# Logits in a shared pool of six PSUM buffers, a third buffer of normalized tokens, and a new order of the pieces

## The chip, the cores and the metric

The kernel runs on one core of one Trainium2 chip. The metric is the time of one execution on the device in microseconds (us); lower is better. Times are medians of several runs of the same kernel. A profile is one further execution, recorded by the hardware; its span runs from the first to the last instruction.

Engine names in this text: PE multiplies matrices, DVE works on vectors, ACT evaluates functions and evicts PSUM, POOL (GpSimd) and SP mostly issue DMAs here. PSUM is the memory that PE writes.

## The reference

A transformer block on one sequence of S = 2048 tokens of width D = 640: a layer norm, then local dilated attention and an MLP side by side, and everything is added to the input.

```python
def _A_ref(x, wqkv, wo):
    H = 32; Dh = D // H                       # Dh = 20
    W, dil = 8, 2
    qkv = (x @ wqkv).reshape(B, S, 3, H, Dh)  # then transposed
    q, k, v = qkv[0], qkv[1], qkv[2]
    idx = pos[:, None] - (jnp.arange(W) * dil)[None, :]
    mask = idx >= 0
    logits = jnp.einsum("bhsd,bhswd->bhsw", q, kg) * scale   # kg: k at idx
    logits = jnp.where(mask[None, None, :, :], logits, -1e9)
    attn = _softmax(logits, axis=-1)
    o = jnp.einsum("bhsw,bhswd->bhsd", attn, vg)             # vg: v at idx
    return o.reshape(B, S, D) @ wo

def _B_ref(x, w1, b1, w2, b2):                # F = 1536
    h = _gelu(jnp.einsum("bsd,df->bsf", x, w1) + b1)
    return jnp.einsum("bsf,fd->bsd", h, w2) + b2

xn = _layernorm(x)
return x + _A_ref(xn, A_wqkv, A_wo) + _B_ref(xn, B_w1, B_b1, B_w2, B_b2)
```

Every token attends to itself and to the seven tokens 2, 4, ..., 14 places before it.

## The kernel before

**Chunks and blocks.** The 2048 tokens are four chunks (n = 0 to 3) of 512, each of four blocks (j or bl = 0 to 3) of 128. D = 640 is five channel tiles of 128. Most work happens with channels on the partitions and 512 tokens in the free dimension.

**Pieces and the order.** All work is cut into 647 named pieces, small functions that each emit a few instructions on one engine. One long string, ORDER, lists every piece once; the kernel calls them in that order with manual scheduling. So each engine's instruction stream is the sequence of its own pieces as they stand in ORDER, and each engine works through its stream in order. Semaphores make a piece wait for its operands and for the release of the buffer that it writes. An engine that waits holds up all that stands behind it.

**The pieces.** The first digit is the chunk.

- `st`, `su`, `sq`, `ng`, `rs`, `rc`: mean and variance of a block's tokens (DVE in chunks 0 and 1, ACT in 2 and 3), square root on ACT, reciprocal on DVE. `xn{n}{bl}`: the normalized block (L259), on DVE in chunk 0, on ACT after that, written to the pool `lnp`.
- `tp`, `tc0..`: transposes by PE and their copies (chunk 0 only). `tc{n}{bl}` of later chunks: a transposing DMA issued by SP (L292) that writes `xnT`, the normalized tokens with channels on the partitions.
- `ga`, `gb`, `gd`, `ge`, `hj`: q, k, v projections of chunk 0 in parts of 128 or 256 tokens (L349, L380); `gc`, `hc` their evictions by ACT. `pj{n}{which}{to}`: one output tile of q (0), k (1) or v (2) of later chunks, five matmuls of 128x512 (L336); `pc...` its eviction (L400).
- `qk{n}{j}{h}`: on DVE, the products of q with k at four of the eight window offsets (half h) for block j, into the tile `half` (L433). `pa{n}{j}{k}`: DVE folds the five channel tiles to two (KEPT = 2): one fold of 2048 elements (k = 0), one of 1024 (k = 1) (L465).
- `lg{n}`: 16 matmuls with the matrix `head_of` sum the channels of each head into the logits L (L474). `cl{n}`: ACT copies them to SBUF (L486). Softmax: `m`, `mx` (max and subtraction, DVE), `ex` (Exp on ACT), `ss`, `ri`, `at` (sum, reciprocal, product, DVE). `xd{n}{j}`: SP issues a DMA that spreads block j's weights over the channels (L548), to the tile `ax` in even chunks and to a spent part of `x_sb` in odd ones.
- `av{n}{j}{h}`: weights times v (DVE, L557). `aa{n}{j}`: the two halves are added, by an accumulating DMA that POOL issues in chunks 0 to 2 (L567) and by DVE in chunk 3 (L569). `ab`, `ot`: DVE adds the remaining four window offsets into `oT` (L573, L577).
- `f1{n}_{ft}`: a tile of the MLP's first layer, five matmuls of 128x512 (L586); `ge{n}_{ft}`: its Gelu on ACT (L602).
- `o{n}{bl}{pc}`: the output of block bl, in pieces: pc = 0 to 3 are three MLP tiles each, pc = 4 the attention's five tiles (which needs `ot` of that block); each a 512-wide `lo` and a 128-wide `hi` matmul (L622, L624). `oc`: two ACT copies; `od`: POOL issues a DMA that adds the block to the output.
- `xp`: x is written to the output; `xb`: POOL's DMA adds b2 to it; `ldx`, `ld2`, `ldo`: loads of x, w2, wo. `wa`, `wb`: small warming matmuls into a tile `idle`. `tb`, `b1`: b1 is transposed by PE and copied. The last block (33) ends with `oclo`, `ohi`, `ochi`, `ochd`.

**PSUM.** Three pools share it: `psA`, four buffers of 128x512 fp32, in which all projections, f1 tiles and PE transposes take turns; `psL`, one buffer of twice that size for the logits (and for `idle` and `tb` before them); `psO`, one `lo` and one `hi`. A buffer of `psA` is free again when ACT has evicted it.

**Tables.** ACT loads a function table (L173) whenever Sqrt, Gelu or Exp follows another of them.

The lines around the change, in the pools' part:

```python
psA = ctx.enter_context(tc.tile_pool(name="psA", bufs=4, space=bass.MemoryType.PSUM))
psL = ctx.enter_context(tc.tile_pool(name="psL", bufs=1, space=bass.MemoryType.PSUM))
lnp = ctx.enter_context(tc.tile_pool(name="lnp", bufs=2))
```

Of the kernel before, what the change touches and what calls it, by code (L numbers as in the profile page):

```python
# [31 lines left out]

KEPT = (2, 2, 2, 2)
BY_DMA = ((0, 1, 2, 3), (0, 1, 2, 3), (0, 1, 2, 3), ())
CUT = 2560
ACT_STATS = (2, 3)

COLS = ((0, 2), (2, 4), (4, 5))

ORDER = """  # L40
wa ho st00a sum1 st00 rs00 rc00 neg1 sq1 xn00a tp00a wb xn00b tp00b mean1 tc00a rs01 rc01 tb b1 tc00b ga gb2 xn01 tp01
tc01a tc01b gb3 gb4 gd ge gc4 gc1 hj100 st02a st02 rs02 hc100 st03a st03 hj101 gc0 rc02 xn02 rs03 hj102 rc03 xn03
hc101 hc102 tp02 tc02 hj202 tp03 tc03 hj201 hc201 hj010 st11a hc010 st13a hc202 st12a hj012 hc012 hj112 hc112 f10_3
st11 ldx hj011 f10_9 st10a st10 st12 st13 rs1 qk011 ge0_3 rc1 xn13 pad01 qk000 qk001 tc13 ge0_9 xn12 tc12 pa000 qk010
pk hj110 hc110 hj111 hc111 hc011 qk030 qk031 qk021 pad11 xn11 f10_10 tc11 pa010 xn10 qk020 tc10 ge0_10 f10_2 ge0_2
hj200 hc200 f10_0 pa030 f10_6 f10_11 su20 ge0_6 xp2 su22 su23 pj111 pc111 ge0_0 su21 ng2 pj110 pc110 pj104 pc104 sq23
pj120 pc120 ge0_11 sq20 pj114 pc114 pj113 pc113 pa001 pa020 pa021 pj102 pc102 pa031 pa011 lg0 cl0 mask m0 hj212 hc212
pj123 pc123 mx0 ex0 pj103 pc103 pj112 pc112 ss0 ri0 pj101 pc101 pj100 pc100 qk110 qk100 ld2 ldo xb2 sq22 qk130 pj124
pc124 hj211 sq21 qk121 rs2 pj121 pc121 hj210 hc210 rc2 f10_8 qk131 hc211 f11_9 ge1_9 xp0 xn20 f10_1 ge0_1 f10_7 tc20
f11_5 xb0 qk120 xn21 tc21 qk101 ge1_5 ge0_7 xn23 tc23 ge0_8 xn22 qk111 o000 f11_8 ge1_8 pa130 at0 pa110 f11_0 ge1_0  # L50
pa100 pad12 f10_5 ge0_5 f11_3 ge1_3 f11_6 su32 tc22 pa120 pa101 xd00 f10_4 su33 pj214 pc214 pa111 su31 su30 pj210
pc210 pad21 xd02 ge0_4 pj211 pa121 ge1_6 pa131 lg1 pj200 pad02 av000 av001 aa00 pc200 ng3 sq32 sq31 sq30 av020 pc211
av021 xd01 av011 o001 pj213 pc213 pj122 pj202 pc202 av010 o002 ab00 ot00 pj204 pj212 o003 pc212 pj223 pj222 cl1 aa02
xd03 pc122 av030 av031 m1 mx1 sq33 rs3 pj201 rc3 pc204 o004 oc00 ab02 ot02 pj224 ex1 o020 aa01 aa03 ss1 ri1 xn33 at1
ab01 ot01 ab03 o021 o022 o023 o024 xp1 tc33 pc201 xn32 tc32 pc222 oc02 ot03 od02 f12_7 xd10 av101 pad22 xd12 pc223
f11_4 xn30 o030 o031 o032 o033 pc224 xd11 xn31 pj221 av100 aa10 o034 oc03 f11_2 o010 ge1_4 tc31 av120 o011 o012 o013
o014 av110 av111 aa11 ge2_7 pc221 od03 f11_7 ge1_7 pj203 pc203 ge1_2 xd13 f11_1 av131 tc30 pj311 pc311 av130 aa13
pj304 f12_3 ge2_3 pj310 pc310 pc304 ge1_1 pj302 av121 aa12 ab10 ot10 f11_10 pc302 ge1_10 pj313 pc313 qk201 qk200 pj312
pj314 ab11 ot11 qk210 pc312 oc01 od01 f13_8 ge3_8 qk211 o130 ab13 pa200 pc314 f11_11 ge1_11 qk231 f12_6 o131 ot13
qk230 xb3 f12_0 ge2_0 pj220 pc220 o132 o133 o134 oc13 pj301 pc301 pa210 ge2_6 ab12 ot12 qk221 pj300 pj324 pc300 qk220  # L60
f13_7 xb1 pc324 od13 pa211 pj303 o120 pa230 pa220 pa231 pc303 pad31 pa221 pa201 lg2 ge3_7 cl2 qk301 f12_2 m2 mx2 ex2
f13_10 f12_8 ge2_8 o121 o122 o123 od00 o124 oc12 qk310 ss2 pj320 pc320 qk311 ri2 at2 xd22 xd20 o110 o111 qk331 o112
o113 o114 oc11 od11 qk330 f13_6 ge3_6 f12_5 ge2_5 ge3_10 o100 ge2_2 qk320 pa330 qk321 pa320 f13_5 f12_4 ge3_5 pj322
f13_2 o101 ge2_4 qk300 xd21 pc322 pa321 o102 o103 o104 ge3_2 pa300 pa301 pa331 pa310 pa311 lg3 f13_3 av210 f13_9 oc10
od10 od12 av211 aa21 ge3_3 f12_10 ge2_10 xd23 av230 av200 f12_1 ge2_1 ge3_9 av231 aa23 f12_9 ge2_9 f13_1 ge3_1 f13_4
f12_11 av201 av221 ab21 ge3_4 av220 pj321 o210 o211 o212 f13_0 ot21 ge2_11 o213 o214 f13_11 cl3 m3 mx3 ex3 pad32 ss3
ri3 at3 xd32 oc21 o200 o201 pc321 o202 aa20 ab20 ot20 ab23 ot23 ge3_0 aa22 o203 o310 o204 oc20 pj323 pc323 ab22 ot22
av320 o230 o231 o232 o233 o234 od20 oc23 av321 aa32 xd30 o311 o312 od21 ab32 o220 o221 o222 o223 o224 ge3_11 xd31
av311 od23 o313 av301 av310 oc22 od22 o320 o321 o322 o323 av300 ot32 o324 oc32 aa31 ab31 ot31 o314 oc31 o300 o301 o302
xd33 od32 aa30 o330 o303 ab30 ot30 o304 av331 av330 aa33 ab33 o331 o332 o333 ot33 od31 xl o334 oclo oc30 ohi ochi ochd  # L70
od30
""".split()


# [1 line left out]
def kernel(  # L76
# [16 lines left out]
    nc = tc.nc  # L93
# [5 lines left out]

    consts = ctx.enter_context(tc.tile_pool(name="consts", bufs=1))  # L100
    wts = ctx.enter_context(tc.tile_pool(name="wts", bufs=1))
    psA = ctx.enter_context(tc.tile_pool(name="psA", bufs=4, space=bass.MemoryType.PSUM))
    psL = ctx.enter_context(tc.tile_pool(name="psL", bufs=1, space=bass.MemoryType.PSUM))
    psO = ctx.enter_context(tc.tile_pool(name="psO", bufs=1, space=bass.MemoryType.PSUM))
    lnp = ctx.enter_context(tc.tile_pool(name="lnp", bufs=2))
    stp = ctx.enter_context(tc.tile_pool(name="stp", bufs=4))
    xtp = ctx.enter_context(tc.tile_pool(name="xtp", bufs=3))
    qkvp = ctx.enter_context(tc.tile_pool(name="qkvp", bufs=2))
# [9 lines left out]
    wqkv = [wts.tile([P, KT, D], BF16, name=f"w{s}_sb") for s in "qkv"]  # L118
# [6 lines left out]
    wqkv_v = A_wqkv.rearrange("(t p) n -> p t n", p=P)  # L125
# [6 lines left out]
    def load_w(s):  # L132
        nc.sync.dma_start(wqkv[s][:], wqkv_v[:, :, s * D : (s + 1) * D])
# [43 lines left out]
    mask = consts.tile([H, W, MW], BF16, name="mask")  # L177
# [16 lines left out]
    acc = consts.tile([P, NCH * BPC], F32, name="acc")  # L194
# [3 lines left out]
    tiles = {}  # L198
# [216 lines left out]
    half = prodp.tile([P, BPC, 2, W // 2, KT, P], BF16, name="half")  # L415
# [22 lines left out]
        )  # L438

    ones = nc.const_aps.tensor(1.0, [P, CH], BF16)  # L440
    idle = psL.tile([P, W, P], F32, tag="L", name="idle")

    def do_warm(n, cols):

        for _ in range(n):
            nc.tensor.matmul(
                idle[:].rearrange("p w c -> p (w c)")[:, 0:cols],
                lhsT=ones[:, 0:P],
                rhs=ones[:, 0:cols],
                start=True,  # L450
                stop=True,
            )
# [8 lines left out]
    def do_pa(n, j, k):  # L461

        a, b = ((slice(0, 2), slice(2, 4)), (slice(0, 1), slice(1, 2)), (slice(0, 1), slice(4, 5)))[k]
        kept, gone = (half[:, j, :, :, ts, :].rearrange("p h w t c -> p (h w) t c") for ts in (a, b))
        nc.vector.tensor_tensor(out=kept, in0=kept, in1=gone, op=ALU.add)  # L465

    def do_lg(n):
        L = psL.tile([P, W, P], F32, tag="L", name="L")
        tiles["L", n] = L
        ts = {KT: range(KT), 3: (0, 1, 4), 2: (0, 4), 1: (0,)}[KEPT[n]]  # L470
        for t in ts:
            for h in range(2):
                for j in range(BPC):
                    nc.tensor.matmul(  # L474
                        L[j * H : (j + 1) * H, W // 2 * h : W // 2 * (h + 1), :],
                        lhsT=head_of[:],
                        rhs=half[:, j, h, :, t, :],
                        start=(t == ts[0]),
                        stop=(t == ts[-1]),
                        skip_group_check=True,  # L480
                    )

    def do_cl(n):
        Lb = smp.tile([P, W, P], BF16, tag="Lb", name="Lb")
        tiles["Lb", n] = Lb
        nc.scalar.copy(Lb[:], tiles["L", n][:])  # L486

    def do_mask():
        Lb = tiles["Lb", 0]
# [74 lines left out]
    def do_aa(n, j):  # L564
        a, b = (half[:, j, h].rearrange("p w t c -> p (w t c)") for h in range(2))
        if j in BY_DMA[n]:
            nc.gpsimd.dma_start(a, b, accum_op=ALU.add, max_dma_last_dim=CUT)  # L567
        else:
            nc.vector.tensor_tensor(out=a, in0=a, in1=b, op=ALU.add)  # L569

    def do_ab(n, j):
        a, b = half[:, j, 0, 0:2], half[:, j, 0, 2:4]
        nc.vector.tensor_tensor(out=a, in0=a, in1=b, op=ALU.add)  # L573

    def do_ot(n, j):
        oT = get(("oT", n), lambda: otp.tile([P, KT, CH], BF16, tag="oT", name="oT"))
# [106 lines left out]
    piece("sum1", do_su, 0, 1)  # L683
    piece("neg1", do_ng, 0, 1, 2)
    piece("wa", do_warm, 1, P)
    piece("wb", do_warm, 2, P)
    piece("sq1", do_sq, 0, 1)
    piece("ga", do_ga, 0, 2)
# [99 lines left out]
```

## Time and profile before

| | |
|---|---|
| median of 3 runs | 207.28 us (207.03 to 208.06) |
| the profiled execution | 207.49 us, of which the span is 205.7 us |
| granted TensorE clock | 1.000 |
| DVE's longest groups | products `qk` 46.2 us (32 of 1.482), `av` 45.6 (32 of 1.485), folds `pa` 29.6, `ab` 13.1 |
| ACT's longest groups | Gelu 32.2 us (48 of about 0.685), casts of the projections 26.0, table loads 15.4 (12 of 1.283) |
| DMA queues | 31.77 MB, mean 154 GB/s |

The busy shares say how long an engine worked, not whether it set the time; the waits say who stood still for whom; the chain names, from the last instruction backwards, what each step had waited for. DVE's and ACT's instructions overlap at their ends: a product lasts 1.48 us, but the next one starts 1.40 us after it. For sums along an engine the distance from start to start is used. PE's 128x512 matmuls last 0.379 us each in the records and start every 0.216 us.

### The profile page before, as it was taken

Reading aid. Unit: us, or ns where it says so; the run is one execution under the profiler, and the core shown is the slowest. Engines: PE = TensorE matmul, PEld = TensorE weight load, DVE = VectorE, ACT = ScalarE, POOL = GpSimd, SP = SyncE. Lnnn points to the kernel's source line nnn. Section 1 sums busy time; section 2 is a strip of 40 time slices with the busy share of each in tenths; the row PEclk is TensorE's granted clock in tenths of the full one; section 3 lists DMA queues with packets and bytes.
Section 4 is the critical chain, followed back from the end, with each engine's and each line's share of the span. In section 5 each row is a group of like instructions: output and inputs, shape, how many; then the busy total and the mean of one; then the engine's idle time right before and its main releaser. Section 6 shows DMA issues by size and latency. Waiting matters only on the chain.

```text
span 205.7 us, 3262 instructions
## 1 busy us (share of the span) xinstructions
PE 200.8 (98%) x1285; PEld 112.2 (55%) x1285; DVE 175.4 (85%) x214; ACT 127.7 (62%) x242; POOL 34.4 (17%) x49
## 2 busy tenths in 40 slices
PE   7899999999999999999999999999999999999994
PEld 2797745565445555555555554555444555555552
DVE  3489999379998989949999994999979979799981
ACT  5488999899999879916466344834616854221210
POOL 2000000050000422102703303001023420311210
DMA  6999389969258599899996965018209998931244
GB/s 210 390 397 370 75 232 326 403 102 185 64 116 264 99 186 181 142 192 124 207 198 113 144 107 64 0 16 182 41 0 132 162 193 162 192 41 17 30 52 64
DMA packets 27335, 31.77 MB, mean 154 GB/s; under 512 B 9272, under 2 KB 22072, under 8 KB 27320
## 3 DMA queue, kind: packets, MB, share of 16 engines
q0 software_dynamic: 7408, 12.78, 39.4%
q1 hardware_dynamic: 19600, 18.58, 31.4%
q8 instruction: 10, 0.16, 0.3%
q10 hardware_dynamic: 312, 0.20, 0.3%
q14 instruction: 5, 0.04, 0.1%
HBM read 10.00 MB, written 7.54 MB: 85 GB/s over the span
## 4 chain that ended last, share of the span: by engine, by line
PE 95%; DMA 3%; SPq 0%; DVE 0%; issue 0%
PE lo L622 29%; PE hps L586 25%; PE pps L336 24%; PE hi L624 7%; PE gps L380 7%; DMA wq_sb<-in_A_wqkv_dram 3%; PE L L474 2%; PE gps L349 1%; PE tp L280 0%; SPq L130 0%; DVE osb L652 0%
## 5 line engine op out<-in xcount | busy, mean ns | idle before, releaser
L586 PE MATMUL hps<-xnT,w_sb 128*128 128x512 bf16 x240 | 55.6, 379 | 0.0
L433 DVE TENSOR_TENSOR half<-qT,kT 128x2560 bf16<-128x2560 bf16 x32 | 46.2, 1482 | 2.9 <-PE L L474 2.8
L622 PE MATMUL lo<-w_sb,hT 128*128 128x512 bf16 x144 | 41.3, 379 | 0.0
L586 PEld LDWEIGHTS <-w_sb 128*128 128x128 bf16 x240 | 22.9, 98 | 26.3 <-issue 0.8
L629 ACT CAST osb<-lo 128x512 bf16<-128x512 f32 x15 | 8.8, 587 | 36.8 <-PE hi L624 18.5
L624 PE MATMUL hi<-w_sb,hT 128*128 128x128 bf16 x144 | 31.5, 219 | 0.0
L602 ACT ACTIVATE hT<-hps,b1T 128x512 bf16<-128x512 f32 x36 | 24.0, 683 | 10.7 <-PE hps L586 10.7
L465 DVE TENSOR_TENSOR half<-half 128x2048 bf16<-128x2048 bf16 (+1 forms) x32 | 29.0, 952 | 0.2
L635 POOL DMA_DIRECT2D out_dram<-osb x15 | 13.6, 973 | 77.1 <-ACT osb L630 68.5
L557 DVE TENSOR_TENSOR half<-vT,x_sb 128x2560 bf16<-128x2560 bf16 x16 | 22.8, 1485 | 4.4 <-DMA x_sb<-e 3.0
L557 DVE TENSOR_TENSOR half<-vT,ax 128x2560 bf16<-128x2560 bf16 x16 | 22.8, 1485 | 2.3 <-PE L L474 1.4
L622 PEld LDWEIGHTS <-hT 128*128 128x128 bf16 x144 | 14.1, 98 | 16.8
L622 PE MATMUL lo<-wo,oT 128*128 128x512 bf16 x80 | 23.1, 379 | 0.0
L567 POOL DMA_DIRECT2D half<-half x12 | 14.3, 1195 | 48.9 <-DVE half L557 48.5
L336 PE MATMUL pps<-xnT,wv_sb 128*128 128x512 bf16 x75 | 18.5, 379 | 0.0
L336 PE MATMUL pps<-xnT,wq_sb 128*128 128x512 bf16 x75 | 18.3, 379 | 0.0
L336 PE MATMUL pps<-xnT,wk_sb 128*128 128x512 bf16 x75 | 17.7, 379 | 0.0
L624 PE MATMUL hi<-wo,oT 128*128 128x128 bf16 x80 | 16.9, 219 | 0.0
L173 ACT ACT_TABLE_LOAD x12 | 15.4, 1283 | 0.9 <-PEq L772 0.7
L624 PEld LDWEIGHTS <-hT 128*128 128x128 bf16 x144 | 14.1, 98 | 2.2
L573 DVE TENSOR_TENSOR half<-half 128x1280 bf16<-128x1280 bf16 x16 | 13.1, 820 | 1.3 <-DMA half<-half 1.2
L622 PEld LDWEIGHTS <-oT 128*128 128x128 bf16 x80 | 7.8, 98 | 9.4
(91 smaller groups left out, 263.7 us busy)
## 6 DMA issues: line engine op xcount, KB each, us to landing
half<-half POOLq DMA_DIRECT2D x12, 640.0 KB, 7.1
w_sb<-in_B_w_dram SPq DMA_DIRECT2D x4, 960.0 KB, 11.0
out_dram<-osb POOLq DMA_DIRECT2D x15, 160.0 KB, 4.0
ax<-e SPq DMA_DIRECT2D x8, 256.0 KB, 4.8
x_sb<-e SPq DMA_DIRECT2D x8, 256.0 KB, 4.8
out_dram<-b2bc POOLq DMA_DIRECT2D x3, 640.0 KB, 8.7
x_sb<-in_A_x_dram SPq DMA_DIRECT2D x1, 1280.0 KB, 12.9
out_dram<-x_sb SPq DMA_DIRECT2D x2, 640.0 KB, 8.7
```

The lines of the kernel that those rows point to most:

```text
L173: nc.scalar.activation(warm[:], nc.const_aps.tensor(0.0, [P, 1], F32), func)
L336: nc.tensor.matmul(ps[:], lhsT=wqkv_p[which][:, ti, to, :], rhs=xnT[:, ti, :], start=(ti == 0), stop=(ti == KT - 1),)
L380: nc.tensor.matmul(ps[:, to - a, :], lhsT=wqkv_p[which][:, ti, to, :], rhs=tiles["xnT", 0][:, ti, pair * 2 * P : (pair + 1) * 2 * P], star ...
L433: nc.vector.tensor_tensor(out=half[:, j, h], in0=q[:, :, at].unsqueeze(1).to_broadcast([P, W // 2, KT, P]), in1=window(k, h, at), op=ALU.mult,
L465: nc.vector.tensor_tensor(out=kept, in0=kept, in1=gone, op=ALU.add)
L557: nc.vector.tensor_tensor(out=half[:, j, h], in0=window(qkv_tile(n, 2), h, cs), in1=ax_view(n)[:, j, ws, :].unsqueeze(2).to_broadcast([P, ...
L567: nc.gpsimd.dma_start(a, b, accum_op=ALU.add, max_dma_last_dim=CUT)
L586: nc.tensor.matmul(ps[:], lhsT=w1_sb[:, ti, ft * P : (ft + 1) * P], rhs=tiles["xnT", n][:, ti, :], start=(ti == 0), stop=(ti == KT - 1),)
L602: nc.scalar.activation(hT, tiles["hps", n, ft][:], ACT.Gelu_apprx_tanh, bias=b1T[:, ft : ft + 1], scale=1.0)
L622: nc.tensor.matmul(lo[:], lhsT=lhs, rhs=rhs[:, 0:CH], start=first, stop=last)
L624: nc.tensor.matmul(hi[:, 0 : D - CH], lhsT=lhs, rhs=rhs[:, CH:D], start=first, stop=last)
L635: nc.gpsimd.dma_start(rows, tiles["osb", n, bl][:], accum_op=ALU.add)
```

## The change

Four things change.

1. `psL` is gone. `psA` has six buffers, and the logits take two of them, one for each half h of the window. `lg` runs over h outermost (before: over the channel tile), and `cl` copies each half by itself. `idle` and `tb` come from `psA` too.
2. `lnp`, the pool of normalized blocks, has three buffers where it had two.
3. ORDER is another permutation of the same pieces.
4. Some code is written otherwise to the same effect: `ab` flattens its operands; `AB_DMA` and `PA_DMA` could send folds to DMAs, but are empty; the load of the q weights is a loop of one step. KEPT is (2, 2, 2, 2) as before.

```diff
-    psA = ctx.enter_context(tc.tile_pool(name="psA", bufs=4, space=bass.MemoryType.PSUM))
-    psL = ctx.enter_context(tc.tile_pool(name="psL", bufs=1, space=bass.MemoryType.PSUM))
+    psA = ctx.enter_context(tc.tile_pool(name="psA", bufs=6, space=bass.MemoryType.PSUM))
     psO = ctx.enter_context(tc.tile_pool(name="psO", bufs=1, space=bass.MemoryType.PSUM))
-    lnp = ctx.enter_context(tc.tile_pool(name="lnp", bufs=2))
+    lnp = ctx.enter_context(tc.tile_pool(name="lnp", bufs=3))
...
-    idle = psL.tile([P, W, P], F32, tag="L", name="idle")
+    idle = psA.tile([P, CH], F32, tag="acc", name="idle")
...
-        tiles["tb"] = psL.tile([P, 2 * W * P], BF16, tag="L", name="tb")
+        tiles["tb"] = psA.tile([P, 2 * CH], BF16, tag="acc", name="tb")
...
     def do_lg(n):
-        L = psL.tile([P, W, P], F32, tag="L", name="L")
-        tiles["L", n] = L
+        tiles["L", n] = [psA.tile([P, W // 2, P], F32, tag="acc", name=f"L{h}") for h in range(2)]
         ts = {KT: range(KT), 3: (0, 1, 4), 2: (0, 4), 1: (0,)}[KEPT[n]]
-        for t in ts:
-            for h in range(2):
+        for h in range(2):
+            for t in ts:
                 for j in range(BPC):
                     nc.tensor.matmul(
-                        L[j * H : (j + 1) * H, W // 2 * h : W // 2 * (h + 1), :],
+                        tiles["L", n][h][j * H : (j + 1) * H, :, :],
...
-        nc.scalar.copy(Lb[:], tiles["L", n][:])
+        for h in range(2):
+            nc.scalar.copy(Lb[:, W // 2 * h : W // 2 * (h + 1), :], tiles["L", n][h][:])
...
     def do_ab(n, j):
-        a, b = half[:, j, 0, 0:2], half[:, j, 0, 2:4]
-        nc.vector.tensor_tensor(out=a, in0=a, in1=b, op=ALU.add)
+        a, b = (half[:, j, 0, w : w + 2].rearrange("p w t c -> p (w t c)") for w in (0, 2))
+        if j in AB_DMA[n]:
+            nc.gpsimd.dma_start(a, b, accum_op=ALU.add)
+        else:
+            nc.vector.tensor_tensor(out=a, in0=a, in1=b, op=ALU.add)
```

Of ORDER, some stretches in the new order (a line of "..." leaves out pieces):

```
ldx pad02 tb st00a wb st00 sum1 ho rs00 rc00 neg1 sq1 rs01 xn00a tp00a xn00b tp00b wa tc00a mean1 ga tc00b gb2 rc01
...
ge1_9 qk111 qk100 xn21 tc21 f10_4 qk121 pa120 pa121 f11_8 ge0_7 f10_5 pc124 xn22 ge1_3 f10_1 ge0_1 tc22 ge1_8 f11_5
...
pa100 qk110 ge0_4 pa110 pa111 pa131 pa101 lg1 cl1 av000 pj220 pc202 pj211 pc211 pj221 su33 su30 ng3 av001 aa00 xd02
...
pad21 o003 f12_11 sq31 rs3 pj122 pc122 m1 mx1 pj201 pc201 rc3 o004 oc00 av030 aa03 ex1 ab02 ot02 ss1 ri1 xn31 xn30
tc30 at1 xd10 ab01 ot01 pj212 pc212 xd11 ab03 ot03 pc223 o020 o021 o022 o023 o024 oc02 f12_7 pad22 o030 o031 o032 o033
xn32 pj222 xn33 xl av100 av101 od00 aa10 o034 pj203 xd13 av130 od02 oc03 o010 o011 o012 av110 pc222 av111 aa11 pc220
pc203 f11_7 ge1_7 o013 o014 tc31 tc32 f11_1 ge1_1 av131 tc33 pj311 pj310 pc310 xd12 pj303 av120 pc303 oc01 od01 av121
aa12 ab10 ot10 f12_5 ge2_11 f11_11 pc221 pj313 pc313 qk201 pj320 f12_0 pc311 ge2_5 pj304 pc304 qk200 pc320 pa200 pj302
...
ge2_6 o124 oc12 od12 m2 qk301 mx2 ex2 qk300 pj324 pc324 ss2 ri2 pj224 pc224 o110 o111 o112 o113 pa300 pa301 o114 oc11
od11 at2 xd23 xd21 qk310 pa310 f13_6 ge3_6 xd20 f12_3 ge2_3 qk321 f12_10 pa311 o100 o101 o102 xd22 pa320 o103 o104
oc10 pa321 f12_2 f13_8 pa330 pa331 ge2_10 lg3 cl3 av210
...
oc32 o300 o301 o302 od32 o303 o304 oc31 av330 oc30 o331 o332 o333 od31 aa33 ab33 ot33 o334 oclo ohi ochi od30 ochd
```

The same stretch of the order before, from the exponential of chunk 1 to its products, for comparison:

```
xd03 pc122 av030 av031 m1 mx1 sq33 rs3 pj201 rc3 pc204 o004 oc00 ab02 ot02 pj224 ex1 o020 aa01 aa03 ss1 ri1 xn33 at1
ab01 ot01 ab03 o021 o022 o023 o024 xp1 tc33 pc201 xn32 tc32 pc222 oc02 ot03 od02 f12_7 xd10 av101 pad22 xd12 pc223
f11_4 xn30 o030 o031 o032 o033 pc224 xd11 xn31 pj221 av100 aa10 o034 oc03 f11_2 o010 ge1_4 tc31 av120 o011 o012 o013
o014 av110 av111 aa11 ge2_7 pc221 od03 f11_7 ge1_7 pj203 pc203 ge1_2 xd13 f11_1 av131 tc30 pj311 pc311 av130 aa13
```

## The prediction

> **What bounds the kernel now.** I read the busy shares and the shares of the chain that ended last, then the waits of PE alone, then the chain in order of time.
>
> ```profile
> PE 200.8 (98%) x1285; PEld 112.2 (55%) x1285; DVE 175.4 (85%) x214; ACT 127.7 (62%) x242; POOL 34.4 (17%) x49
> ...
> PE 95%; DMA 3%; SPq 0%; DVE 0%; issue 0%
> ```
>
> ```profile
> PE tp L280 <- DVE xn L265: 0.8, 1, 0.8
> PE idle L446 <- PEq L772: 0.8, 1, 0.8
> PE gps L349 <- DMA wq_sb<-in_A_wqkv_dram: 0.6, 1, 0.6
> ```
>
> ```profile
> 1.20 5.51 DMA wq_sb<-in_A_wqkv_dram
> 6.76 1.03 PE gps L349 x15
> ...
> 202.00 0.96 PE hi L624 x17
> 202.99 0.29 DVE osb L652
> ```
>
> PE waits three times in the whole run, 2.2 us together, and all three lie before 6.76 us, where the first q projection finds its weights. From there to 202.95 PE is never idle. So the span is 6.76 (load), 196.2 (matmuls back to back) and 2.8 (last eviction and store). No order of the same matmuls makes the middle shorter; the new one can only open holes in it. The question is whether every matmul still finds its operand and its PSUM buffer in time.
>
> **The change, part by part.** The matmuls are the same in number and form: 0 us. The head: `tb` now stands before the first transposes on PE and waits for b1, whose last descriptor lands at 5.24; xn00a ends at 5.38 and wq lands at 6.71, so the start stays 6.76: 0, bounds 0 and +0.3 (b1 later by as much). The tail (o334, ohi, ochi, its store) is unchanged: 0. Eviction of the logits, from the groups of instructions:
>
> ```profile
> L486 ACT CAST Lb<-L 128x1024 bf16<-128x1024 f32 x4 | 4.0, 1012 | 0.8 <-PE L L474 0.8
> L400 ACT CAST qT<-pps 128x512 bf16<-128x512 f32 x15 | 8.7, 588 | 2.6 <-PE pps L336 2.6
> ```
>
> One cast of 1.012 becomes two of 0.588: 0.16 us more ACT time per chunk, but with h outermost the first half is complete after 8 of 16 matmuls, 0.49 us sooner (16 take 0.98). It lies on the softmax chain and gains some 0.3 us there; PE sees none of it, because the next chunk's products cover it.
>
> The order: I place each matmul piece by the row it had, plus the pieces that moved ahead of it, minus those that moved behind. One f1 or pj piece is 5 matmuls in 1.08, an o piece of three is 0.81, five gps matmuls are 0.55. lg1: 63.85 + 2 x 1.08 - 0.81 = 65.2. pj311: 100.95 - 1.08 = 99.87. o134: 119.32 + 3 x 1.08 = 122.56. lg2: 126.98 + 2 x 1.08 - 0.81 = 128.33. lg3: 151.90 + 1.08 = 152.98. o334 stays at 200.76. Against each I set the work of the engine that feeds it, with the start-to-start steps of the DVE rows (product 1.40, or 1.52 where the next instruction needs it; first fold 1.14 or 1.25; second fold 0.61; ab and ot 0.86 and 0.41, 0.52 if needed next).
>
> lg0 and lg1 keep their room: DVE has the last fold at about 36.3 against 37.0, and 64.7 against 65.2. The tightest stretch is chunk 1's softmax. These are SP's and then DVE's timelines there:
>
> ```profile
> 82.66 2.60 SPq L292 DMA_TRANSPOSE xnT<-xn  x2
> 85.35 3.25 SPq L548 DMA_DIRECT2D x_sb<-e  x3
> 88.69 2.76 SPq L292 DMA_TRANSPOSE xnT<-xn  x1
> 91.50 0.58 SPq L548 DMA_DIRECT2D x_sb<-e  x1
> 92.14 2.48 SPq L292 DMA_TRANSPOSE xnT<-xn  x1
> ```
>
> ```profile
> 84.36 0.69 DVE L531 TENSOR_TENSOR e<-e,rs 128x1024 bf16<-128x1024 bf16 x1
> ...
> 90.58 9.90 DVE L557 TENSOR_TENSOR half<-vT,x_sb 128x2560 bf16<-128x2560 bf16 x7 [3.01 <-DMA x_sb<-e]
> ...
> 128.12 1.49 DVE L433 TENSOR_TENSOR half<-qT,kT 128x2560 bf16<-128x2560 bf16 x1 [2.83 <-PE L L474]
> ```
>
> The attention weights of a chunk go out in four spreads (xd); DVE stands still for 3.01 us until the first has landed. Before, three spreads, one transpose, the fourth spread, one transpose. New: xd10, xd11, xd13, then three transposes (tc31, tc32, tc33), and only then xd12. ex1 comes 0.96 later (o004 ends at 79.4 instead of 78.5, then table load and warm), so at1 ends at 86.0. SP then issues the three spreads (3.34 with the gaps) until 89.4. Three transposes at the rows' 2.76, 2.48 and, with no spread in flight any more, 1.22 (the shortest issues) end near 96.0; bounds 3 x 1.2 and 3 x 2.76, so 93.1 to 97.7. xd12 lands 4.8 later (median of the spreads; 3.5 to 6.2): 100.8, bounds 96.6 to 103.9. DVE starts chunk 1's products when xd10 lands, 86.05 + 5.2 = 91.3, and needs xd12 after six of them, at 99.7. It waits 1.1, bounds 0 and 4.2. From there to the end of pa201 the steps sum to 27.1: 126.8 plus the wait, 127.9, against lg2 at 128.33. So 1.5 us of the wait is free and the slack absorbs it: 0 on PE, bounds 0 and +2.7. pj311 needs tc33 (issued near 94.8, 2.4 to 5.9 to landing, so 97.2 to 100.7) at 99.87: 0, bounds 0 and +0.8, not additive, since a late PE gives DVE the same time back.
>
> On this queue the Trainium skill speaks against the row: "DMA: Bandwidth & Descriptors", Issuing engines are not separate DMA queues, calls the time a sequencer takes to start a DMA usually small relative to the DMA itself. By that, xd12 would be out by 90 and nothing would wait. The rows show 1.2 to 2.8 us per transpose issue against 2.4 to landing, so the sum goes by the rows.
>
> After lg2 the chain is: oc12 at 136.2, 0.75 for its two casts, 1.40 to the Exp, 1.06 for it, then DVE from ss2 to the end of pa331, 13.3: 152.8 against lg3 at 152.98. Nearly a tie. The other DVE meetings have 0.5 us or more (ot21 166.4 against o214 166.9; ot22 184.6 against o224 185.2), and ot33 comes 3 us before o334 (1.5 before). The accumulating DMAs (aa) are issued at about the old distance from their readers: 0.
>
> PSUM: six buffers carry what four and a dedicated pair did. I checked each matmul piece against the eviction that frees its buffer, with ACT laid out the same way. Closest: f10_1 at 55.38 behind ge0_7 ending at 55.27, pj220 0.15 after pc200, pj313 0.2 after ge2_11, o030 0.1 after oc02, hj010 0.2 after tc03, all 0 if the rows hold. For six such meetings and lg3 I allow 0.3 us in all, 0.05 each, an estimate: the casts' starts scatter that much behind the matmuls. Bounds 0 and +1.2 (below). The third buffer of normalized tokens only lets ACT write a third block before the first has been transposed: 0, since PE has 1.08-us pieces to run meanwhile.
>
> Sum: 205.7 + 0.3 = 206.0 of span; with the 1.8 us around it (this execution took 207.49) 207.8. It was 0.2 above the median of 207.28, so against the median 207.6.
>
> **The rivals.** SP's queue decides (slower): the three transposes keep 2.76 each because the spreads are still in flight, and xd12 lands at 97.7 + 5.2 = 102.9. DVE waits 3.2, pa201 ends at 130.0, lg2 is 1.7 late; it decides from a landing after 101.2. Time 207.3 + 0.3 + 1.7 = 209.3. For it: both transposes behind a spread took 2.5 to 2.8. Against: the pair with none ahead took 2.60 together.
>
> ACT becomes the bound through the shared buffers (slower): from ge0_2 at 20.5 to 55.3 ACT has some 60 rows with hardly a gap, and it meets f10_1 with 0.1 us to spare. If its rows run 3% longer than laid out, that is 1.0 us there, and PE stands it out: 208.6. It decides from 0.1 us. For it: ACT is above 80% busy in the slices to 55 us. Against: in the kernel before, meetings of 0.1 to 0.2 us cost PE nothing.
>
> The clock drops (slower): the fourteen warm matmuls at the start take 3.87 us where warm steps would give 10 x 0.216 + 4 x 0.055 = 2.4. A hole that cools the array costs such a 1.5: 207.6 + 1.5 = 209.1. Against: the longest hole above is under 3 us, and the granted clock is 1.000 although PE paused three times at the start. The Trainium skill, "TensorE: Matmul & The Clock Gate", A second HAM failure mode, describes a kernel whose cycling through PSUM banks made PE idle briefly and often until the clock fell back. No run here shows it.
>
> Faster: only what lies outside the 196.2 us can shrink. If the start came when xn00's transposes are copied, at 6.6, it would save 0.2; beyond 1.0 nothing in the rows offers it.
>
> **How the numbers follow.** A measurement of this kernel can tell about 0.5% (1.04 us) from no change. Forecast, no hole over 1 us: 0.63, own range 206.9 to 208.3. SP's queue 0.16, ACT 0.12, clock 0.03, faster 0.05; the last 0.01 is a mishap I don't see, put with slower. That gives slower 0.32, same 0.63, faster 0.05. The range reaches from 206.9 (nothing lost, low end of the scatter) to 209.2, which takes in ACT's case and most of the queue's.
>
> **What would show it.** Right: PE's waits are still the three at the start, each later one below 0.3; xd12's issue stands behind three transposes at 95 to 97; DVE waits near 100 for a spread and lg2 starts at 128.3 to 128.6; PE ends near 203. Wrong: a wait of PE for half at lg2 or lg3 of over 1 us, waits for casts or for xnT summing to 1 us, 128x512 matmuls longer than 379 ns, or a first projection well off 6.76.

## The result and the profile after

| | before | after |
|---|---|---|
| median | 207.32 us (206.99 to 208.06, 6 runs) | 209.83 us (209.16 to 210.58, 6 runs) |
| ratio | | 1.0116, 95% interval 1.0097 to 1.0135 |
| the profiled execution | 207.49 us, span 205.7 us | 209.45 us (one of the six), span 207.6 us |
| granted TensorE clock | 1.000 | 1.000 |

The change made the kernel 1.2% slower, 2.5 us by the medians. In this and the later runs the ratios leave out single executions over 1.5% above the fastest of their kernel (214.21, 214.52 and 213.34 us in three of the later kernels); medians and ranges count them. The two profiled executions lie 1.9 us of span apart; the rest is that the one of after lies 0.4 below its median and the one of before 0.2 above. So the trace has to explain 1.9 us.

The busy shares of the kernel after, and the shares of the chain that ended last:

```profile
PE 202.1 (97%) x1285; PEld 112.4 (54%) x1285; DVE 176.6 (85%) x214; ACT 127.0 (61%) x246; POOL 34.6 (17%) x49
...
PE 74%; DVE 12%; ACT 7%; DMA 4%; issue 2%; SPq 0%; DVEq 0%
```

Before, 95% of the chain was PE. Now it leaves PE for a quarter of the span. PE's waits in the kernel after (who waits for whom: us in total, times, the longest):

```profile
PE lo L631 <- DVE oT L586: 1.4, 1, 1.4
PE idle L449 <- PEq L781: 0.8, 1, 0.8
PE L L479 <- DVE half L471: 0.3, 1, 0.3
PE gps L352 <- DVE mv L240: 0.2, 1, 0.2
```

Two of them are new and lie in the stretch where PE used to run without a gap: an output projection (o134) that waits for `ot13`, and the logits lg2 that wait for DVE's last fold. From the starts of the matmuls, the holes are 1.53 us ahead of o134 (122.54 to 124.07), 0.34 at lg2 and 0.27 at pj100 (a transpose that lands at 30.42). The first q projection starts 0.18 sooner than before (6.58; its weights landed at 6.34). Together 1.53 + 0.34 + 0.27 - 0.18 = 1.96: the whole difference, to 0.1 (the spans differ by 1.85, the two times by 1.96).

Where the chain turns off is seen in the same chain in order of time (start, length, what):

```profile
94.34 0.21 SPq L295
94.56 0.05 issue
94.61 8.33 DMA x_sb<-e
102.94 0.02 issue
102.96 0.04 DVE half L563
103.00 1.37 issue
104.37 1.48 DVE half L563
```

One spread of the attention weights, issued at 94.61, takes 8.33 us to land. SP's timeline of the kernel after says which (start, length, what, how many):

```profile
84.50 1.99 SPq L295 DMA_TRANSPOSE xnT<-xn  x1
86.59 3.24 SPq L554 DMA_DIRECT2D x_sb<-e  x3
89.87 4.69 SPq L295 DMA_TRANSPOSE xnT<-xn  x3
94.61 1.73 SPq L554 DMA_DIRECT2D x_sb<-e  x1
```

It is xd12, behind three transposes. And DVE's timeline there (in brackets the idle time before, and who ended it):

```profile
91.21 8.50 DVE L563 TENSOR_TENSOR half<-vT,x_sb 128x2560 bf16<-128x2560 bf16 x6 [0.60 <-DMA x_sb<-e]
102.96 2.89 DVE L563 TENSOR_TENSOR half<-vT,x_sb 128x2560 bf16<-128x2560 bf16 x2 [3.25 <-DMA x_sb<-e]
```

DVE makes six products, stands still for 3.25 us until xd12 is there, and everything behind it on DVE is that much late. About 1.4 us of it is slack; 1.53 + 0.34 reach PE.

Why 8.33, where the kernel before had no spread above 6.2? The view of the DMA queues, for the kernel after from 96.6 to 100 us and then from 100 to 103 (packets, MB, share of the 16 engines; q0 carries GpSimd's transfers, q1 SyncE's):

```profile
q0 software_dynamic: 259, 0.66, 101.8%
q1 hardware_dynamic: 148, 0.03, 5.4%
```

```profile
q1 hardware_dynamic: 142, 0.26, 59.7%
q0 software_dynamic: 174, 0.23, 45.4%
```

POOL's timeline has the accumulating transfer aa10 (640 KB), first in the kernel before, then in the kernel after, where the output rows od02 (160 KB) follow it:

```profile
93.77 1.20 POOL L567 DMA_DIRECT2D half<-half  x1 [7.52 <-DVE half L557]
```

```profile
94.40 1.20 POOL L573 DMA_DIRECT2D half<-half  x1 [10.81 <-DVE half L563]
95.11 1.44 POOL L644 DMA_DIRECT2D out_dram<-osb  x1
```

So POOL issued aa10 at 94.40, 0.2 us ahead of xd12; before, it came 2.3 us behind the last spread (91.50). Until 100 us its 0.66 MB have the engines nearly to themselves (packets overlap, so a share can pass 100%); SyncE's queue moves 0.03 MB. Only then come the 0.26 MB of xd12. That is a reading; the experiments test it.

### The profile page after: what moved, and what is told of

It reads as the page before. It is cut to its first block, busy times and chain, and to the rows that moved or that the text cites. A ratio compares the mean times of both kernels' runs of the same rounds, so it can differ in the third digit from the quotient of the medians.

```text
span 207.6 us, 3272 instructions
## 1 busy us (share of the span) xinstructions
PE 202.1 (97%) x1285; PEld 112.4 (54%) x1285; DVE 176.6 (85%) x214; ACT 127.0 (61%) x246; POOL 34.6 (17%) x49
## 4 chain that ended last, share of the span: by engine, by line
PE 74%; DVE 12%; ACT 7%; DMA 4%; issue 2%; SPq 0%; DVEq 0%
PE lo L631 25%; PE pps L339 16%; PE hps L595 15%; PE hi L633 6%; DVE half L436 6%; PE gps L383 5%; DMA x_sb<-e 4%; DVE half L471 4%; PE idle L449 2%; PE L L479 2%; ACT xn L266 2%; DVE half L582 1%; PE gps L352 1%; ACT hT L611 1%; ACT trash L224 1%
## 5 line engine op out<-in xcount | busy, mean ns | idle before, releaser
L631 PE MATMUL lo<-w_sb,hT 128*128 128x512 bf16 x144 | 40.7, 379 | 0.0
L471 DVE TENSOR_TENSOR half<-half 128x2048 bf16<-128x2048 bf16 (+1 forms) x32 | 29.5, 953 | 0.5
L644 POOL DMA_DIRECT2D out_dram<-osb x15 | 14.3, 996 | 71.0 <-ACT osb L639 71.0
L339 PE MATMUL pps<-xnT,wq_sb 128*128 128x512 bf16 x75 | 17.7, 379 | 0.1
```

Source lines behind the costliest of these rows:

```text
L339: nc.tensor.matmul(ps[:], lhsT=wqkv_p[which][:, ti, to, :], rhs=xnT[:, ti, :], start=(ti == 0), stop=(ti == KT - 1),)
L631: nc.tensor.matmul(lo[:], lhsT=lhs, rhs=rhs[:, 0:CH], start=first, stop=last)
L644: nc.gpsimd.dma_start(rows, tiles["osb", n, bl][:], accum_op=ALU.add)
```

## The experiments

Two theories stood at the start. Theory 1: the order of SyncE's queue, with xd12 last and just behind aa10. Theory 2: the shared pool of six banks with the logits in two tiles. The steps named are pieces of ORDER; a moved piece changes its place in its engine's queue, and its instructions stay the same.

### The spread ahead of the transposes; past one transpose only

```diff
-xn32 pj222 xn33 xl av100 av101 od00 aa10 o034 pj203 xd13 av130
+xn32 pj222 xn33 xl av100 av101 od00 aa10 o034 pj203 xd13 xd12 av130
...
-tc33 pj311 pj310 pc310 xd12 pj303 av120
+tc33 pj311 pj310 pc310 pj303 av120
```

> The changed kernel with one step moved: the spread xd12 goes ahead of the three transposes tc31, tc32, tc33 on SyncE's queue, straight behind xd13. Theory 1 (xd12 is issued last, behind three transposes and just behind the accumulating transfer aa10; av120 waits for its landing, and TensorE pays at o134 and lg2): xd12 is issued near 89.9 instead of 94.61 and lands near 94 to 95 instead of 102.94, VectorE's wait of 3.2 us before av120 is gone, o134 and lg2 start without a hole, and the time is 209.8 - 1.53 - 0.34, about 207.9. Theory 2, the rival (the shared pool of six banks and the logits cut into two tiles make TensorE late, and VectorE's wait is slack): the wait goes and the time stays, 209.5 to 210.

Measured: 211.93 us (210.49 to 214.21), ratio 1.0206, interval 1.0166 to 1.0246. Slower still, and neither theory had that. PE's waits and SP's timeline of this kernel:

```profile
PE pps L339 <- DMA xnT<-xn: 2.8, 1, 2.8
PE idle L449 <- PEq L781: 0.8, 1, 0.8
```

```profile
84.80 2.10 SPq L295 DMA_TRANSPOSE xnT<-xn  x1
87.00 4.88 SPq L554 DMA_DIRECT2D x_sb<-e  x4
91.92 6.83 SPq L295 DMA_TRANSPOSE xnT<-xn  x3
```

The first half of the forecast holds: xd12 lands at 95.58, DVE's wait is gone, and so are the holes at o134 and lg2. But now the last transpose, tc33, is last on the queue, issued at 95.70 behind aa10 (95.06); it lands 7.1 us later at 102.82, and PE waits for it at pj311 (due near 99.9). The wait was handed on.

```diff
-tc31 tc32 f11_1 ge1_1 av131 tc33 pj311 pj310 pc310 xd12 pj303
+tc31 tc32 f11_1 ge1_1 av131 xd12 tc33 pj311 pj310 pc310 pj303
```

> The changed kernel with the spread xd12 moved past one transpose only, between tc32 and tc33 on SyncE's queue, so that it is issued near 93.0, some 1.4 us ahead of the accumulating transfer aa10 (issued 94.40). Theory 1a (xd12 lands late because its packets wait for all of aa10's on the 16 DMA engines): it lands near 97 to 98, before av120 wants it (99.7), VectorE's wait is gone, about 207.9. Theory 1b (only its place on the queue counts): it lands earlier by what it is issued earlier, 1.6, so near 101.3; VectorE still waits 1.6, TensorE loses 0.2 to 0.4 of the 1.87, about 208.3 or more. Theory 2 (pool and cut logits): 209.5 to 210.

Measured: 210.04 us (209.03 to 214.52), ratio 1.0123, interval 1.0085 to 1.0162. xd12, issued at 92.95 with aa10 at 94.14, lands at 96.56: 3.6 us, as theory 1a said (1b: 101.3). tc33, issued at 93.66, lands 7.9 us later at 101.59, and PE waits 2.4 for it. The time (about 207.9 was forecast) was wrong for the same reason as in the run before: I had not asked what is last next.

### The code without the order

```diff
-ldx pad02 tb st00a wb st00 sum1 ho rs00 rc00 neg1 sq1 rs01 xn00a tp00a xn00b tp00b wa tc00a mean1 ga tc00b gb2 rc01
+wa ho st00a sum1 st00 rs00 rc00 neg1 sq1 xn00a tp00a wb xn00b tp00b mean1 tc00a rs01 rc01 tb b1 tc00b ga gb2 xn01 tp01
...
```

> The changed kernel's code (six shared banks, logits in two tiles, three buffers of normalized tokens) with the written order of the kernel before. Theory 1 (the order of the spreads): as fast as before, 207.0 to 207.6. Theory 2 (pool and cut logits): TensorE waits for banks in the old order too, 209 or more. If both have a part, it lies between, near 208.4.

Measured: 207.2 us (207.01 to 209.56), ratio 1.0006, interval 0.9982 to 1.0031. Theory 2 falls. Six shared banks, the cut logits and the third buffer cost nothing in the old order, so the 2.5 us come with the new one. That they cost nothing together with the new order either is shown by the run without aa10 below, which has both.

### The kernel before, with its last spread later

```diff
-pj203 pc203 ge1_2 xd13 f11_1 av131 tc30 pj311
+pj203 pc203 ge1_2 tc30 xd13 f11_1 av131 pj311
```

> The kernel before with one step moved: the transpose tc30 goes ahead of the spread xd13 on SyncE's queue, so that the fourth spread is issued near 94, just behind the accumulating transfer aa10 (issued 93.77) instead of 2.3 ahead of it (91.50). Nothing of the shared pool is in it. Theory 1: xd13 lands near 102 instead of 95.81, av131 (which ran at 97.6) waits some 4.5, the second chunk's logits lose their margin of 1.69 and come 2 to 3 late, 209.2 to 210.2. Theory 2 (pool and cut logits are to blame): VectorE's slack takes the wait, 207.3 to 207.8.

Measured: 207.12 us (206.95 to 209.94), ratio 1.0002, interval 0.9987 to 1.0017. The forecast of theory 1 (209.2 to 210.2) missed, but where the two transfers can be seen, the edit did not do what it was made for. In its profiled execution av100 started 1.9 us later than before, aa10 moved with it to 95.66, and xd13 (94.67) was still 1.0 us ahead; it landed at 98.42, after 3.75 us. That execution is the slowest of the thirteen (209.94 us): its first q projection came at 7.42 instead of 6.76, the granted clock was 0.50 from 7.86 to 11.27 us, and everything behind ran some 2 us late. Which of the two transfers goes first in the other twelve is not shown, so this run decides nothing.

### aa10 moved, and aa10 left out

```diff
-av101 od00 aa10 o034 pj203 xd13 av130 od02 oc03 o010 o011 o012 av110 pc222 av111 aa11 pc220
+av101 od00 o034 pj203 xd13 av130 od02 oc03 o010 o011 o012 av110 pc222 av111 aa11 aa10 pc220
```

> The changed kernel with one step moved on GpSimd's queue: the accumulating transfer aa10 (640 KB) goes behind aa11, so that it is issued near 99.8 instead of 94.40 and is not on the 16 DMA engines when the last items of SyncE's queue are (tc33 issued 93.33, xd12 issued 94.61). SyncE's queue is untouched. Theory 1a (what is issued last on SyncE, spread or transpose, lands 7 to 8 us after its issue because aa10's 640 KB go first; the two kernels with xd12 moved forward only handed this to tc33): xd12 lands near 98.6 instead of 102.94, tc33 near 96, av120 starts without a wait at 99.7, o134 and lg2 have no hole, about 207.9. Theory 1b (the issue times on SyncE alone are to blame): the landing stays near 102 and the time near 209.8. In either case ab10 may wait for aa10 up to 1.5 us on VectorE, in front of ot10.

Measured: 214.88 us (214.49 to 215.25), ratio 1.0365, interval 1.0342 to 1.0387. The landing came as theory 1a has it: xd12, issued at 96.62 with no aa10 about, lands at 100.20, 3.6 us later, and DVE runs through its products. The time came out 7 us wrong, because aa10, now queued behind aa11, itself landed 8.9 us after its issue (100.73 to 109.61), and DVE's next instruction needs it. DVE's waits in this stretch:

```profile
DVE half L582 <- DMA half<-half: 6.1, 2, 5.8
DVE half L563 <- DMA x_sb<-e: 1.4, 1, 1.4
```

I had allowed 1.5 us for the first line. It can't be used to price the change; leaving the transfer out can.

```diff
     def do_aa(n, j):
+        if (n, j) == (1, 0):
+            return
```

> The changed kernel without the transfer aa10: the halves of the second chunk's first prompt are not added, so its output is not the reference's there. Everything on SyncE stays. It takes one suspected cost away by itself. Theory 1a (aa10's 640 KB go ahead of the fourth spread on the 16 DMA engines): xd12 is issued near 94.6 as before and lands near 98 to 98.6 instead of 102.94; VectorE does not wait at av120, o134 and lg2 have no hole: 209.8 - 1.9, about 207.9. If what delays xd12 is the transposes ahead of it and not aa10, it lands near 102 and the time stays at 209.8.

Measured: 207.53 us (206.98 to 207.99), ratio 1.0008, interval 0.9991 to 1.0024. SyncE's queue has the changed kernel's order, three transposes ahead of xd12 and all, and xd12 is issued even later, at 96.11; yet it lands at 99.60, 3.5 us after. The DMA queues of this kernel from 96.1 to 99.6 us show SyncE's alone:

```profile
q1 hardware_dynamic: 661, 0.39, 60.3%
```

DVE's eight products run in one stretch, and PE loses nothing at o134 and lg2:

```profile
92.30 11.31 DVE L563 TENSOR_TENSOR half<-vT,x_sb 128x2560 bf16<-128x2560 bf16 x8 [1.37 <-DMA x_sb<-e]
```

With this transfer gone, the loss of the new order is within the error of nothing. One more thing moved with it: od02, which stands behind aa10 on POOL's queue, went out at 86.25 instead of 95.11 (in the run with aa10 behind aa11, at 86.83). It is not the cause: in the kernel after, the 0.66 MB up to 100 us are aa10's 640 KB alone, and od02 lands at 103.79, later than xd12.

### The third buffer

```diff
-    lnp = ctx.enter_context(tc.tile_pool(name="lnp", bufs=3))
+    lnp = ctx.enter_context(tc.tile_pool(name="lnp", bufs=2))
```

> The changed kernel with two buffers of normalized tokens instead of three. Tells what the third buffer does for the new order: with two, xn32 waits on ScalarE for the landing of tc30 (89.08) and xn33 for another transpose (94 or later), while ScalarE's queue stands, so kv copies and gelus of that stretch come 3 to 5 us late and TensorE waits for banks. Expected if the new order needs it: 2 to 6 us slower than the changed kernel, 212 to 216. If the third buffer is idle weight: 209.8, the same.

Measured: 214.43 us (213.99 to 215.32), ratio 1.0349, interval 1.0321 to 1.0377. The new order needs the third buffer: with two, ACT waits twice for the landing of a transpose before it may write the next block, 3.7 us the longer time, and its copies for PE are late (ACT's wait from 85 to 100 us, then PE's longest three in the whole run; the 2.6 us lie in that stretch, the two others near 26 and 58 us, behind further such waits of ACT of 2.9 and 1.1 us):

```profile
ACT xn L266 <- DMA xnT<-xn: 7.2, 2, 3.7
```

```profile
PE lo L631 <- ACT osb L638: 2.6, 1, 2.6
PE hps L595 <- ACT qT L398: 1.6, 1, 1.6
PE hps L595 <- ACT hT L611: 1.1, 1, 1.1
```

### An earlier start for SyncE's queue

```diff
-ex1 ab02 ot02 ss1 ri1 xn31 xn30 tc30 at1 xd10
+ex1 ab02 ot02 ss1 ri1 xn31 tc31 xn30 tc30 at1 xd10
...
-o013 o014 tc31 tc32 f11_1
+o013 o014 tc32 f11_1
```

> The changed kernel with one step moved: the transpose tc31 is issued right behind xn31, ahead of tc30. Its input is ready at 83.66, and SyncE's queue stands idle until 84.50, when tc30's input comes. Theory 1c (the length of SyncE's queue of four transposes and four spreads is fixed, some 12 us; the kernel before starts it at 82.66 with two transposes ahead of the spreads, the changed one at 84.50 with one, so its last item is issued behind aa10 instead of ahead of it): tc33 is issued near 92.3 and xd12 near 93.5, ahead of aa10's 94.4; xd12 lands near 97 to 98, both under what waits for them (99.7 and 99.8), no hole at pj311, o134 and lg2, about 207.9. If a start some 1 us earlier is not enough, one of the two is late still: 208.5 to 209.8. Theory 2 (TensorE is late for another reason): 209.8.

Measured: 207.98 us (207.32 to 209.28), ratio 1.0042, interval 1.0021 to 1.0064: the time as forecast, and 1.85 below the changed kernel. SP's timeline, in an execution of 208.73 us, 0.75 above the median:

```profile
83.73 4.45 SPq L295 DMA_TRANSPOSE xnT<-xn  x2
88.27 2.60 SPq L554 DMA_DIRECT2D x_sb<-e  x3
90.97 3.77 SPq L295 DMA_TRANSPOSE xnT<-xn  x2
94.79 1.35 SPq L554 DMA_DIRECT2D x_sb<-e  x1
```

The way there differs from the forecast. The holes did not go: PE still waits 0.3 us each at o134 and at lg2. The queue did not end sooner (94.79 against 94.61); the three spreads landed later, which put DVE's first products and with them aa10 at 95.32. So xd12 went from 0.2 behind aa10 to 0.5 ahead of it, and landed at 100.09, 5.3 us after its issue. DVE still waits 1.7 for the third spread.

### The changed queue in the old order

The first try moved xd13 behind av131, which therefore multiplied with what the tile held before, and xd13 had to wait for it.

```diff
-pc201 xn32 tc32 pc222
+pc201 xn32 pc222
...
-pc224 xd11 xn31 pj221
+pc224 xd11 xn31 tc32 pj221
...
-ge1_2 xd13 f11_1 av131 tc30 pj311
+ge1_2 f11_1 av131 tc30 xd13 pj311
```

> The shared pool, cut logits and third buffer with the order of the kernel before (207.2), and in it two steps moved so that SyncE's queue has the changed kernel's form: one transpose, three spreads, three transposes, the fourth spread (tc32 behind xn31, xd13 behind tc30). Theory 1: the fourth spread is issued near 93.5 to 94.5, behind aa10 (92.67), and lands near 101 to 102; av131, due at 96.5, waits 4 to 5 us on VectorE, the second chunk's logits lose their margin of 2.5 and come 1.5 to 2.5 late: 208.7 to 209.8. If the bunching on this queue is not the cause: 207.0 to 207.5.

Measured: 213.4 us (212.67 to 215.56), ratio 1.0308, interval 1.0268 to 1.0347. xd13 was issued only at 97.01, DVE waited 7.2 us and PE 3.7. It serves to size the next run, in which the last lines of the diff read:

```diff
-ge1_2 xd13 f11_1 av131 tc30 pj311
+ge1_2 tc30 xd13 f11_1 av131 pj311
```

> The shared pool, cut logits and third buffer with the order of the kernel before (207.2), and SyncE's queue in the changed kernel's form: one transpose, three spreads, three transposes, the fourth spread (tc32 behind xn31, tc30 ahead of xd13, which stays ahead of av131). Theory 1: xd13 is issued near 93.3 to 93.8, behind aa10 (near 91.6), and lands near 100.5 to 101.5; av131, due at 95.5, waits 5 to 6 us. Of the wait of 7.2 us in the run with xd13 behind av131, 3.7 came through to TensorE at the second logits; so 1.5 to 2.5 here: 208.7 to 209.7. If the bunching is not the cause: 207.0 to 207.5.

Measured: 208.93 us (208.59 to 209.27), ratio 1.0073, interval 1.0047 to 1.0100. Issue, landing, both waits and the time came out as expected. Timelines of SP and of DVE, and PE's waits:

```profile
82.20 1.23 SPq L295 DMA_TRANSPOSE xnT<-xn  x1
84.62 2.51 SPq L554 DMA_DIRECT2D x_sb<-e  x3
87.22 6.00 SPq L295 DMA_TRANSPOSE xnT<-xn  x3
93.28 1.08 SPq L554 DMA_DIRECT2D x_sb<-e  x1
```

```profile
88.47 7.12 DVE L563 TENSOR_TENSOR half<-vT,x_sb 128x2560 bf16<-128x2560 bf16 x5 [1.36 <-DMA x_sb<-e]
100.91 4.30 DVE L563 TENSOR_TENSOR half<-vT,x_sb 128x2560 bf16<-128x2560 bf16 x3 [5.32 <-DMA x_sb<-e]
```

```profile
PE L L479 <- DVE half L471: 2.1, 1, 2.1
```

Two moves on SyncE's queue turn the fast order (207.2) into a slow one with the same signature: the last spread at 93.28 behind aa10 (91.66), landing 7.6 us later, a wait on DVE, a wait of PE at the logits.

### Two more repairs

The first of these takes the early transpose and lets DVE want the third spread later; the second adds one step on GpSimd's queue.

```diff
-xd13 av130 od02 oc03 o010 o011 o012 av110 pc222 av111 aa11
+xd13 od02 oc03 o010 o011 o012 av110 pc222 av111 av130 aa11
```

> The changed kernel with tc31 behind xn31 (207.98 in its own run) and, on VectorE's queue, av130 moved behind av110 and av111, so that the spread that landed third (96.59 there) is wanted third last instead of third. Theory 1: VectorE's wait of 1.7 us at av130 goes, the wait at av120 stays at most 1, o134 and lg2 lose their last holes (0.45 and 0.34): 207.2 to 207.6, level with before. If something other than the spreads holds the rest: 208.0.

Measured: 208.16 us (207.31 to 209.02), ratio 1.0034, interval 1.0014 to 1.0053: no better. The holes at o134 and lg2 are gone, but PE has a new wait, and ACT has one just ahead of it (PE's waits, then ACT's from 85 to 112 us):

```profile
PE pps L339 <- ACT hT L611: 1.2, 1, 1.2
```

```profile
ACT osb L638 <- DMA out_dram<-osb: 1.3, 1, 1.3
```

The output rows od02 stand behind aa10 on GpSimd's queue, were issued at 95.81 and landed at 104.85; ACT's copy for oc01 waited for their buffer, the gelu behind it was late, and PE waited for that gelu's bank at pj313.

```diff
-av101 od00 aa10 o034 pj203 xd13 od02 oc03
+av101 od00 od02 aa10 o034 pj203 xd13 oc03
```

> The kernel with tc31 early and av130 behind av111 (208.16), and a third step moved: the output rows od02 (160 KB) go ahead of aa10 on GpSimd's queue. Their copy is ready near 92.6 and aa10's products near 94.8, so aa10 is not held up. In the run without this, od02 was issued behind aa10 at 95.81 and landed at 104.85; ScalarE's copy for oc01 waited 1.31 for that buffer, the gelu behind it came late, and TensorE waited 1.18 at pj313 for the gelu's bank. Theory 1 (what is issued behind aa10 lands late, whatever queue it is on): od02 lands near 96 to 98, both waits are gone, TensorE has no hole over 0.1 between 70 and 200, 207.0 to 207.4, level with the kernel before. If the wait at pj313 has another cause: 208.1.

Measured: 207.95 us (207.24 to 213.34), ratio 1.0038, interval 1.0019 to 1.0056. In the profiled execution, 207.24 us, PE waits for nothing after its start:

```profile
PE idle L449 <- PEq L781: 0.8, 1, 0.8
```

od02 was issued at 86.12 and landed at 90.73 (its copy is ready at 86.1, not at 92.6 as I had put it: it had stood on GpSimd's queue for 9 us behind a transfer that waits for DVE), and both waits are gone. This one execution is level with before. The median is not, and misses the forecast of 207.0 to 207.4; the trace can't show why, since this execution happens to be the fastest of twelve. That the remaining 0.7 us are near ties that some executions miss is a guess; it stays open. No version beat the kernel before. The old order with the new code (1.0006, interval 0.9982 to 1.0031) is level with it.

## Why the prediction was wrong

The forecast was 207.6, range to 209.2; the time is 209.83. Point by point:

- **PE never idle, so that order can only open holes.** Right. The 1.96 us between the traces are holes of PE, all but the 0.18 at the head.
- **Cut logits, shared banks, third buffer at 0.** Right: 207.2 with all three in the old order. The third buffer's zero is a zero only because the order can't do without it; with two the new order takes 214.43.
- **The near ties in PSUM, the tie at lg3, ot21 and ot22.** They held; no wait of PE for an eviction shows in the kernel after, and lg3 has none. One of the listed ties, pj313 behind ge2_11, did give way once ACT was held up (1.2 us in the first of the two last repairs), so they were rightly listed. pj100's 0.27 us was on no list.
- **Three transposes end near 96.0.** They ended at 94.56 and took 2.0, 1.2 and 1.2: a little better than taken.
- **"xd12 lands 4.8 later (median of the spreads; 3.5 to 6.2)".** This step failed: the term for the landing of xd12 was mis-sized, because it took the landing times of the old order for the new one. It landed 8.33 us after its issue, above the longest spread of before; with aa10 left out, it took 3.5. The wait on DVE became 3.25 instead of 1.1, and "the slack absorbs it: 0 on PE" became 1.87. The slack itself was well measured: 3.25 - 1.87 leaves 1.4, against 1.5 in the prediction. The hole opens at o134 first, which the prediction had placed (122.56) without weighing ot13 against it.
- **"The accumulating DMAs (aa) are issued at about the old distance from their readers: 0."** Here lies the cause. I checked these transfers against who reads them, and not against who shares the DMA engines with them. In the kernel before, xd13 went out 2.3 us ahead of aa10 (91.50 and 93.77); in the new order xd12 goes 0.2 behind it. It could be read off the prediction's own layout: products from 91.3 at 1.40 each, aa10 behind the second, so near 94; xd12 near 96.
- **The rival "SP's queue decides".** It had the place (DVE waiting for xd12) and nearly the numbers: a landing at 102.9, a wait of 3.2, 1.7 us on PE, 209.3; measured were 102.94, 3.25 and 1.87. But it came to 102.9 by slow transposes and a usual landing, and the truth is quick transposes and a slow landing; two errors cancel, which is luck. With the right reason it would have been the forecast. The run without aa10 tells the two apart: same queue, xd12 issued 1.5 us later still, no loss.
- **The range to 209.2.** The bounds of the failed term itself held: a landing from 96.6 to 103.9 and 0 to +2.7 on PE take in 102.94 and 1.87. But 207.6 + 2.7 is 210.3, and the rival's own time was 209.3; the range stopped short of both.
- **ACT as the bound, and the clock.** Neither happened in the kernel after: no wait for ACT, granted clock 1.000, 128x512 matmuls at 379 ns. Its longest hole is 1.53 us. The argument that holes under 3 us speak against a falling clock does not hold, though: in other runs the clock fell behind waits of 2.4 and 2.6 us (last section).

How an item of SyncE's queue fared against aa10, from the DMA records of the profiled executions (us):

| kernel | item | issued | aa10 issued | landed | to landing |
|---|---|---|---|---|---|
| aa10 left out | xd12 | 96.11 | none | 99.60 | 3.5 |
| aa10 behind aa11 | xd12 | 96.62 | 100.73 | 100.20 | 3.6 |
| before | xd13 | 91.50 | 93.77 | 95.81 | 4.3 |
| past one transpose | xd12 | 92.95 | 94.14 | 96.56 | 3.6 |
| after | tc33 | 93.33 | 94.40 | 97.56 | 4.2 |
| before | tc30 | 92.14 | 93.77 | 98.00 | 5.9 |
| all three repairs | xd12 | 94.92 | 95.59 | 98.95 | 4.0 |
| early transpose | xd12 | 94.79 | 95.32 | 100.09 | 5.3 |
| early transpose, av130 later | xd12 | 94.52 | 95.10 | 100.13 | 5.6 |
| past one transpose | tc33 | 93.66 | 94.14 | 101.59 | 7.9 |
| after | xd12 | 94.61 | 94.40 | 102.94 | 8.3 |
| spread early | tc33 | 95.70 | 95.06 | 102.82 | 7.1 |
| changed queue, old order | xd13 | 93.28 | 91.66 | 100.89 | 7.6 |

Of these spreads, one issued 0.7 us or more ahead lands in some 4 us, one 0.5 or 0.6 ahead in 5.3 to 5.6, one behind in over 7. The step between 0.6 and 0.7 rests on one run (all three repairs), in which od02 too no longer follows. The transposes follow less neatly: before's tc30, 1.6 ahead, took 5.9, but its issue alone lasted 2.5; and tc30 of the changed queue in the old order, 0.3 behind, took 5.9 as well. Nor is aa10 the only thing that makes a spread late. In the two runs with the early transpose and od02 in its old place, the third spread took 7.1 and 7.0 us, 5.8 and 5.9 us ahead of aa10, and in the first of them no transfer of GpSimd moved meanwhile. What held it is not shown.

The Trainium skill, "DMA: Bandwidth & Descriptors", Issuing engines are not separate DMA queues, says that DMAs from the scalar, sync and gpsimd engines end up on the same 16 engines and interleave there. The first half agrees with the table: it is GpSimd's transfer that SyncE's spread waits for. Of the second the window from 96.6 to 100 us shows little, 0.66 MB of the one queue against 0.03 of the other.

## What to carry to other kernels

Where an order is rewritten, list for each stretch all large transfers in order of issue, whatever engine issues them, and see what is issued just behind the largest; a landing time taken from the old order holds only for the old neighbours. When a late transfer is moved up, ask at once what is last now and when that is due: three of these runs only passed the wait on. And leave the suspected transfer out once: it priced the cause where moving things had blurred it (and see what else moves when it goes).

## What the runs showed of the hardware

The clock can fall behind short holes of PE. In the kernel with xd12 past one transpose PE waits 2.4 us; the profile by windows shows (window, its length, PE busy, granted clock, DMA share, GB/s):

```profile
98.00:101.80 3.80, 1.45 (x9) 1.00 1.16 172
102.74:106.15 3.41, 3.41 (x10) 0.50 0.63 119
106.50:111.00 4.50, 4.50 (x23) 1.00 0.24 20
```

Seven matmuls in a row start 427 ns apart instead of 216, with one step of 389 ahead of them and one of 253 behind: 1.7 us lost, as half the clock for 3.41 us gives. The granted clock fell likewise, to 0.50 for 3.41 us, behind waits of 2.6, 3.7 and 4.9 us (two buffers; the first try of the old order; aa10 behind aa11), each in one execution. It fell once more at the start of the kernel before with its last spread later, where PE, among small matmuls, had waited 0.35 and then 1.2 us:

```profile
4.45:7.86 3.41, 1.86 (x22) 1.00 1.04 370
7.86:11.27 3.41, 3.41 (x36) 0.50 1.06 392
```

It stayed at 1.00 behind waits of 1.4 (after), 2.1 (the changed queue in the old order) and 2.8 (spread early). So a wait of 2.4 us sufficed once where 2.8 did not another time, and a hole can cost 1.7 us more than its length. The Trainium skill, "TensorE: Matmul & The Clock Gate", Part 1: The HAM clock gate (the "warmup" mystery), puts the fall behind at least one idle window of about 3.4 us, with windows that run freely. That the outcome does not follow the length alone agrees; but the waits of 1.2, 2.4 and 2.6 us were shorter than such a window, so here less than a full one was enough.

Also unexpected: the issue of a transpose on SyncE. Straight behind another transpose it mostly took 1.2 to 1.3 us, in the kernel after even with two spreads in flight (the one issued at 92.00, 1.23). Straight behind a plain DMA it took 1.9 us or more in every profile of this case, 2.04 in the kernel after (89.87), 3.35 in the changed queue in the old order (87.22) and 4.19 with aa10 behind aa11 (89.27). Some behind a transpose took as long (3.06 in spread early, at 95.70), so what sets it stays open.
